# Two tile pairs in turn at the ends of the second layer and at the start of the output stage; split weights loaded whole

## The chip, the cores and the metric

The kernel runs on one core of one Trainium2 chip. The metric is device time in microseconds (us). Engines: PE (TensorE, matrix products), ACT (ScalarE), DVE (VectorE), POOL (GpSimd, here used to issue weight loads), SP (SyncE, which issues the other loads and stores). PE reads SBUF and accumulates in PSUM; ACT and DVE read the sums out of PSUM.

## The reference

Three stages in a row, on 1792 tokens (4 batches of 448), everything in float32:

```python
# attention, 48 (batch, head) pairs, seq 448, head_dim 64
scores = q @ k.T / sqrt(64) - log(448)
x = sigmoid(scores) @ v                      # gathered to x: 1792 x 768
# first layer: elementwise maximum of three products, then a projection
h = maximum(maximum(x @ w1, x @ w2), x @ w3) # 1792 x 768
y = h @ w_out                                # 768 x 768
# second layer and output
h2 = y @ w_in                                # 1792 x 1024
e = exp(h2 - max(h2)); solu = h2 * e / sum(e)
ln = (solu - mean) / sqrt(var + 1e-6) * g_ln # per token
out = ln @ w_out2                            # 1024 -> 768
```

The kernel multiplies `w_out @ w_in` once beforehand, so the second layer is one product of h with a 768 x 1024 matrix.

## The kernel before

**Products.** Each float32 operand is split into a high and a low half of a shorter format (a copy that rounds, then a subtraction), and each product is three matmuls: high x high, high x low, low x high. On top of that every large product uses the seven-product form of a 2 x 2 block multiplication: the left operand gives A11, A12, A22 and the combinations S1 to S4, the right one B11, B21, B22 and T1 to T4, and `PROD` (line 38) says which pair makes P1 to P7. The split right operands ("weights") are written to DRAM early (`w_d`, `w2_d`) and read back later.

**Stages.** First attention and the preparation of the weights, then the first layer in units of nine-matmul products (line 643), then the second layer, called L, then the output stage, called O. L and O each have seven *pairs* p = 0 to 6; a pair is two tiles of 128 tokens. In L a pair is 7 products of 9 matmuls with 512 columns, in O 7 products of 12 matmuls with 384 columns (line 909). L needs seven weights of 1.57 MB (`wf`, in order of use B11, B21, T2, T1, T3, T4, B22), O seven of the same size (`w2t`). They share SBUF slots, so an O weight can be loaded only when the last L pair has used the L weight in its slot (`release`, lines 1024 to 1029). O's B11 has a slot of its own and is loaded early.

**Operands of a pair.** `prep` (line 771) is a generator that makes the seven left operands of a pair step by step: ACT makes each high half (line 51), DVE each low half (line 56) and the sums and differences (line 59). The order is A11, A12, S2, S1, S3, A22, S4, the order in which P1, P2, P6, P5, P7, P4, P3 need them. They live in a ring of ten slots; an L operand takes one slot, an O operand two, and a slot is free once PE has used what lies in it. L's operands come from the rows of h in DRAM (`load_h`, on SP), O's from `u_d` (`load_u`, on SP).

**The order of products.** The loop of line 1058 does one pair after another: P1 of the new pair, then P4 and P3 of the pair before (`close`), then P2, P6, P5, P7 of the new one. P1, P6, P7 and P4 of a pair go into the same PSUM tile X: after each, ACT copies X out (lines 1065, 1109, 1115, 1044) before the next may add to it. P5 and P3 share V, P2 has Z. DVE adds the copies up (line 934 in L, line 59 in O).

**After an L pair** comes `solu_ln` (line 939): two Exp on ACT, two products on DVE, two Squares on ACT, a chain of small steps between ACT and DVE, two scalings on ACT (line 973), two transposes on DVE (line 977), and stores to `u_d`. O's pair p needs the result for p. `load_u(p)` also insists that pair p+1 is through.

**The written order.** PE, ACT, DVE and, late in the kernel, POOL run in program order; each executes its instructions in the order in which the program emits them. A planner decides where the side work goes (lines 880 to 922): each matmul earns credit (0.227 in L, 0.174 in O, line 906), each emitted step costs its planned time, and while credit is positive steps are taken from `bg` (the preps) and, if that has none, from `lazy` (the solu_ln). `charge` books the evacuations. Two places ignore credit: `product_c` takes prep steps until its operand exists, and `load_u` takes lazy steps until the pair is through:

```python
while t not in turned or (p + 1 < NP2 and tiles[2 * p + 3] not in turned and p > 0):
    assert step(lazy), t
```

**Weight loads.** POOL loads each L weight in three pieces of 0.5 MB and each O weight in four of 0.4 MB. Before each piece, `paced` (line 729) lets POOL copy a few values (line 732) of the piece issued three before, which makes POOL wait until that has landed. `w_d` rows are 4 KB per chunk.

**PSUM** has 2 tiles Z, 2 X, 2 V (lines 627 to 629).

Of the kernel before, what the change touches and what calls it, by code (L numbers as in the profile page):

```python
# [15 lines left out]
P = 128  # L16
# [28 lines left out]
def sigmoid_attention_max_moe_solu_ln(tc, q, k, v, w123, wo, wi, w2, g, out):  # L45
# [582 lines left out]
    px_cm, ps_x = open_pool("ps_x", 2, space=PSUM)  # L628
# [122 lines left out]
    spent, cops = set(), {}  # L751
# [18 lines left out]

    def prep(kind, p, a11, a12, a21, a22, s1, view, cost):
        ready = {}

        def high(nm, src):
            parts = halves_of((kind, p, nm))
            while parts is None:
# [3 lines left out]
            copy(act, view(parts[0]), src)  # L780

        def low(nm):
            src, parts = ready.pop(nm)
            rest(dve, view(parts[1]), src, view(parts[0]))
# [4 lines left out]
        yield from high("A12", a12)  # L789
        low("A11")  # L790
        yield cost
        tt(s1, a21, a22, ALU.add)
# [5 lines left out]
        tt(a11, s1, a11, ALU.subtract)  # L798
# [4 lines left out]
        yield from high("S1", s1)  # L803
        low("S2")
        yield cost
        yield from high("S3", a21)
        low("S1")
        yield cost
        yield from high("A22", a22)
        low("S3")  # L810
        yield cost
        yield from high("S4", a12)
        low("A22")
        yield cost
        low("S4")
        yield cost

    def prep_l(p):
        a = [hts.pop((p, i, k)) for i in range(2) for k in range(2)]
        s1 = f_tile(*FIN[8 + p % 2], f"s1_{p}")[:, :HU]  # L820
# [4 lines left out]
    for n, u in enumerate(units):  # L825
# [8 lines left out]
        if old is not None:  # L834
# [4 lines left out]
            if old["u"] == (NG - 1, 1):  # L839
# [14 lines left out]
        if n == len(units) - 1:  # L854
            bg.append(prep_l(0))
# [5 lines left out]
        if u == (NG - 1, 1):  # L861
# [6 lines left out]
            flow.extend(hts[(0, i, k)][:, :8] for i, k in ((1, 1), (0, 1), (1, 0)))  # L868
# [70 lines left out]
    def solu_ln(p):  # L939
# [4 lines left out]
        for i, t in enumerate(pair):  # L944
# [3 lines left out]
            yield 0.2  # L948
# [6 lines left out]
        for i in range(2):  # L955
            c = slice(i, i + 1)
            act.activation(e[i], h[i], AF.Square, bias=su[:, c], scale=-float(F2), accum_out=vs[:, c])
            yield 0.2
# [12 lines left out]
        for i in range(2):  # L971
            c = slice(i, i + 1)
            act.activation(h[i], h[i], AF.Identity, bias=nb[:, c], scale=s1[:, c])
            yield 0.2
# [16 lines left out]
    def prep_o(p):  # L991
# [6 lines left out]
        s1 = tp.tile([P, 4, P], F32, tag="s1", name=f"os1_{p}", bufs=1).rearrange("p k (i t) -> p k i t", i=4)  # L998
        return prep("O", p, *a, s1, lambda t: t.rearrange("p (k i t) -> p k i t", k=4, i=4), 0.69)

    spare = [("e", None)] * 3 + FIN[:4] + FIN[10:]
# [29 lines left out]
    def close(o):  # L1031

        kind, p = o["kind"], o["p"]
        e1, u2, u3, cx = o["at"]
# [8 lines left out]
        else:  # L1043
            act.copy(cx, o["X"])
            put_out(p, 1, 0, cx)
        product_c(o["V"], kind, p, "P3", False, True)
# [10 lines left out]
    stage = [("L", p) for p in range(NP2)] + [("O", p) for p in range(NP2)]  # L1057
    for n, (kind, p) in enumerate(stage):
        w = 512 if kind == "L" else HU
        at = targets(kind, p)  # L1060
        e1, u2, u3, cx = at
        X = ps_x.tile([P, 512], F32, tag="x", name=f"X{n}")[:, :w]
        product_c(X, kind, p, "P1", True, False)
        release(kind, p, "P1")
        act.copy(e1, X)
# [12 lines left out]
        else:  # L1078
            close(old)
        if n == 3:  # L1080
            load_w2(LOADS[0], 7)
        if 0 < n < NP2 - 1:
            load_h(p + 1, 0)
            load_h(p + 1, 1)
        if NP2 - 1 <= n + 1 < len(stage) - 1:
            load_u(n + 2 - NP2)
# [99 lines left out]
```

## Time and profile before

| | us |
|---|---|
| median of 3 runs (lowest, highest) | 705.95 (705.54, 709.5) |
| the profiled execution | 706.08 |
| its span, first to last instruction | 704.3 |
| PE busy | 656.2 (93%) |
| DVE busy | 491.4 (70%) |
| ACT busy | 372.7 (53%) |
| POOL busy | 83.2 (12%) |
| mean granted clock of PE | 0.966 |

The busy shares are means over stages. A row of a timeline is: start, duration, engine, line, operation, destination <- sources, shapes, count and, in brackets, the idle time of the engine ahead of it and what ended that. Names have no buffer numbers: X, V, Z are PSUM tiles, `wf` an L weight, `w2t` an O weight, c_L and c_O operands of a pair, `h`, `u`, `e`, `cx` the evacuated sums, `a` rows of h.

### The profile page before, as it was taken

Reading aid. Unit: us, or ns where it says so; the run is one execution under the profiler, and the core shown is the slowest. Engines: PE = TensorE matmul, PEld = TensorE weight load, DVE = VectorE, ACT = ScalarE, POOL = GpSimd, SP = SyncE. Lnnn points to the kernel's source line nnn. Section 1 sums busy time; section 2 is a strip of 40 time slices with the busy share of each in tenths; the row PEclk is TensorE's granted clock in tenths of the full one; section 3 lists DMA queues with packets and bytes.
Section 4 is the critical chain, followed back from the end, with each engine's and each line's share of the span. In section 5 each row is a group of like instructions: output and inputs, shape, how many; then the busy total and the mean of one; then the engine's idle time right before and its main releaser. Section 6 shows DMA issues by size and latency. Waiting matters only on the chain.

```text
span 704.3 us, 9779 instructions
## 1 busy us (share of the span) xinstructions
PE 656.2 (93%) x3283; PEld 528.7 (75%) x3283; DVE 491.4 (70%) x1061; ACT 372.7 (53%) x709; POOL 83.2 (12%) x184
## 2 busy tenths in 40 slices
PE   9999999999999999999999998579999958885997
PEld 6555688545569999999999997348888847884997
DVE  4799977797467888868976866227887835654652
ACT  6888333678665554555455533116667714735341
POOL 1111110001001011111011003330001431000000
PEclk9999999999999999999999999869999977988999
DMA  8788688736201556554675349982534797354311
GB/s 282 228 255 256 185 275 307 285 110 221 87 1 48 149 181 211 156 163 153 176 213 165 111 125 328 305 285 67 165 104 121 246 285 250 97 149 137 107 52 68
DMA packets 83201, 125.16 MB, mean 178 GB/s; under 512 B 35792, under 2 KB 62928, under 8 KB 83152
## 3 DMA queue, kind: packets, MB, share of 16 engines
q1 hardware_dynamic: 71344, 70.84, 32.1%
q0 software_dynamic: 11664, 53.49, 24.6%
q8 instruction: 26, 0.43, 0.3%
q14 instruction: 23, 0.19, 0.1%
q10 hardware_dynamic: 144, 0.23, 0.1%
HBM read 84.15 MB, written 40.37 MB: 177 GB/s over the span
## 4 chain that ended last, share of the span: by engine, by line
PE 55%; issue 14%; DMA 13%; DVE 12%; ACT 5%; POOL 1%; SPq 0%; POOLq 0%; DVEq 0%; ACTq 0%
PE x L643 17%; PE v L643 9%; PE av L272 7%; PE X L909 6%; DMA w2tT<-w_d 4%; PE z L643 4%; PE sc L251 4%; PE V L909 4%; DMA wfT<-w_dT 3%; DMA wfB<-w_dB 3%; PE sc L247 2%; PE Z L909 1%; DMA w2tB<-w_d 1%; DVE y_wo L157 1%; DVE wt L59 1%
## 5 line engine op out<-in xcount | busy, mean ns | idle before, releaser
L272 PE MATMUL av<-sf,vr 128*64 128x448 f32 x384 | 77.5, 545 | 0.0
L259 ACT ACTIVATE sf<-sc,bias_s 128x896 f32<-128x896 f32 x72 | 67.8, 1011 | 1.3
L141 POOL DMA_DIRECT2D raw<-in_w x52 | 28.2, 543 | 279.9 <-DVE S L56 140.1
L272 PEld LDWEIGHTS av<-sf,vr 128*64 128x64 f32 x384 | 25.4, 136 | 40.8 <-issue 35.5
L251 PE MATMUL sc<-qt,kt 64*128 64x448 f32 x432 | 52.0, 377 | 3.5 <-ACT sf L256 3.5
L251 PEld LDWEIGHTS sc<-qt,kt 64*128 64x128 f32 x432 | 38.5, 184 | 15.1 <-ACT sf L256 5.9
L472 PE MATMUL pw<-wi_t,r_wo 128*128 128x512 f32 x216 | 49.6, 390 | 0.0
L472 PEld LDWEIGHTS pw<-wi_t,r_wo 128*128 128x128 f32 x216 | 40.4, 188 | 9.3 <-issue 1.0
L683 ACT COPY u<-x 128x448 f32<-128x448 f32 x36 | 19.1, 531 | 43.3 <-PE x L643 43.3
L909 PE MATMUL X<-w2tT,c_O_S 128*128 128x384 f32 x168 | 35.0, 358 | 7.3 <-DMA w2tT<-w_d 7.3
L909 PE MATMUL X<-wfT,c_L_S 128*128 128x512 f32 x126 | 34.8, 420 | 6.7 <-DMA wfT<-w_dT 6.1
L909 PEld LDWEIGHTS X<-w2tT,c_O_S 128*128 128x128 f32 x168 | 31.7, 204 | 8.8 <-DMA w2tT<-w_d 7.2
L59 DVE TENSOR_TENSOR u<-V,u 128x384 f32<-128x384 f32 x14 | 7.8, 557 | 39.6 <-ACT u L1115 28.1
L909 PEld LDWEIGHTS X<-wfT,c_L_S 128*128 128x128 f32 x126 | 24.6, 200 | 14.4 <-DMA wfT<-w_dT 5.4
L643 PE MATMUL x<-T3h,S 128*128 128x448 f32 x108 | 33.7, 366 | 0.0
L643 PE MATMUL x<-B11h,A 128*128 128x448 f32 x108 | 33.7, 366 | 0.0
L643 PE MATMUL x<-T4h,A 128*128 128x448 f32 x108 | 33.6, 365 | 0.0
L643 PE MATMUL x<-T2h,S 128*128 128x448 f32 x108 | 33.6, 365 | 0.0
L643 PE MATMUL v<-B22h,S 128*128 128x448 f32 x108 | 33.6, 365 | 0.0
L643 PE MATMUL v<-T1h,S 128*128 128x448 f32 x108 | 33.6, 365 | 0.0
L643 PE MATMUL z<-B21h,A 128*128 128x448 f32 x108 | 33.6, 365 | 0.0
L412 ACT ACTIVATE raw<-raw,g_sb 128x192 f32<-128x192 f32 x32 | 13.3, 466 | 31.3 <-DVE raw L157 31.3
(187 smaller groups left out, 1597.6 us busy)
## 6 DMA issues: line engine op xcount, KB each, us to landing
raw<-in_w POOLq DMA_DIRECT2D x52, 384.0 KB, 4.1
w_d<-w2s SPq DMA_DIRECT2D x48, 192.0 KB, 2.4
u_d<-e SPq DMA_DIRECT2D x14, 512.0 KB, 2.8
ut<-u_d SPq DMA_DIRECT2D x56, 128.0 KB, 4.0
kr<-in_k SPq DMA_DIRECT2D x24, 256.0 KB, 3.3
vr<-in_v SPq DMA_DIRECT2D x24, 256.0 KB, 3.9
raw<-in_wi POOLq DMA_DIRECT2D x16, 384.0 KB, 4.5
w_dT<-wsT SPq DMA_DIRECT2D x12, 512.0 KB, 3.6
```

Source lines behind the costliest of these rows:

```text
L59: dve.tensor_tensor(out=dst, in0=a, in1=b, op=op)
L141: pool.dma_start(out=t, in_=source(key).rearrange("p (n t) -> p n t", t=2))
L157: dve.scalar_tensor_tensor(out=yi, in0=raws[key][:, cols, 0], scalar=29, in1=yi, op0=ALU.logical_shift_right, op1=ALU.bitwise_or)
L247: pe.matmul(sc[:, 0, :S], lhsT=kt[:, x, c * P :], rhs=qt[:, y], start=start, stop=stop)
L251: pe.matmul(sc[:, j, :S], lhsT=kt[rows, x, c * P : (c + 1) * P], rhs=qt[rows, y], start=start, stop=stop)
L259: act.activation(sf, sc[:, :, :S], AF.Sigmoid, bias=bias_s, scale=1.0 / math.sqrt(D))
L272: pe.matmul(pa[j * D : (j + 1) * D, :S], lhsT=vr[:, j, c], rhs=sf if c == 3 else sf[:, j], start=(n == 0), stop=(n == 3),)
L412: act.activation(half, half, AF.Copy, scale=g_sb[:, kc + 4 * i : kc + 4 * i + 1])
L472: pe.matmul(ps, lhsT=wt[:, a, cols], rhs=wi_t[:, b, c0 : c0 + 512], start=(i == 0), stop=(i == 3 * KC - 1))
L643: pe.matmul(ps, lhsT=l, rhs=r, start=(start and c == 0 and i == 0), stop=(stop and c == 2 and i == 2), skip_group_check=True)
L683: act.copy(e, ps)
L909: pe.matmul(ps, lhsT=hl[l][:, c * P : (c + 1) * P], rhs=wt[:, c, m], start=(start and c == 0 and i == 0), stop=(stop and c == chunks - 1 a ...
```

## The change

- **Pairs in turn.** The loop runs over groups: L (0,1), (2), (3), (4), (5,6) and O (0,1), (2), ... (6). In a group of two, each product is done for both pairs before the next product. The two preps are interleaved (`in_turn`), the first with a lead of 8, 6 or 1 steps. P4 of a group of two comes ahead of the next P1. X has three PSUM tiles.
- **Loads.** Each L weight is one DMA without gates. POOL waits only, by `hold`, for the h rows of pair 0 and of pair 1 before it issues weights behind them. O weights keep their four pieces; POOL waits for the piece four before.
- **load_u** takes one prep step ahead of each forced lazy step, and stands at other places: for pair 1 after P1 of (5,6), pair 2 after P1 of O (0,1), pair 3 after its P5, pairs 4 to 6 after P6 of O 2 to 4.
- **Costs and small things.** ACT steps of `solu_ln` are planned at 0.05 instead of 0.2. The s1 buffer of odd O pairs is two pieces, so its instructions are too. When the ring is full, `high` emits the pending low half before it waits.

```diff
-    px_cm, ps_x = open_pool("ps_x", 2, space=PSUM)
+    px_cm, ps_x = open_pool("ps_x", 3, space=PSUM)
...
-    def paced(out, in_):
-
-        if len(flow) > 2:
-            pool.tensor_copy(gate, flow.popleft())
-        pool.dma_start(out=out, in_=in_)
-        flow.append(out[:, 0, :8])
+    def hold(view):
+
+        pool.tensor_copy(gate, view)
...
-        for c in range(3):
-            paced(t[:, c].bitcast(F32), w_d[nm][:, c, : 2 * 512].rearrange("p (a b) -> p a b", a=2))
+        pool.dma_start(out=t.bitcast(F32).rearrange("p c a b -> p c (a b)"), in_=w_d[nm][:, :, : 2 * 512])
...
         for kc in range(4):
-            paced(t[:, kc].bitcast(F32), w2_d[n][kc][:, off])
+            if len(flow) > 3:
+                hold(flow.popleft())
+            pool.dma_start(out=t[:, kc].bitcast(F32), in_=w2_d[n][kc][:, off])
+            flow.append(t[:, kc, 0, :8].bitcast(F32))
...
+        def high(nm, src, before=None):
             parts = halves_of((kind, p, nm))
+            if parts is None and before:
+                low(before)
+                before = None
+                yield cost
+                parts = halves_of((kind, p, nm))
             while parts is None:
                 yield None
                 parts = halves_of((kind, p, nm))
             ready[nm] = (src, parts)
-            copy(act, view(parts[0]), src)
+            for d, t in pieces(view(parts[0]), src):
+                copy(act, d, t)
+            if before:
+                low(before)
...
+    def in_turn(first, second, lead):
+
+        gens, n = [first, second], 0
+        while gens:
+            for gen in gens[n % 2 :] + gens[: n % 2] if n >= lead else gens[:1]:
+                cost = next(gen, "end")
+                if cost == "end":
+                    gens.remove(gen)
+                    break
+                if cost is not None:
+                    n += 1
+                    yield cost
+                    break
+            else:
+                yield None
...
-                for tag in (2, 3, 4):
-                    load_wf(LOADS[tag], tag)
                 last_rows(1)
                 for k in range(2):
                     load_h(1, k)
+                for k in range(2):
+                    hold(hts[(1, 1, k)][:, :8])
+                for tag in (2, 3, 4):
+                    load_wf(LOADS[tag], tag)
...
-            bg.append(prep_l(0))
+            bg.append(in_turn(prep_l(0), prep_l(1), 8))
...
             act.activation(e[i], h[i], AF.Exp, bias=low[:, c], scale=-1.0, accum_out=ssum[:, c])
-            yield 0.2
+            yield 0.05
...
             while t not in turned or (p + 1 < NP2 and tiles[2 * p + 3] not in turned and p > 0):
+                step(bg)
                 assert step(lazy), t
...
+    groups = [("L", g) for g in ((0, 1), (2,), (3,), (4,), (5, 6))]
+    groups += [("O", g) for g in ((0, 1), (2,), (3,), (4,), (5,), (6,))]
+    prev = None
+    for n, (kind, g) in enumerate(groups):
+        if prev and len(prev) > 1:
+            for o in prev:
+                fourth(o)
+        now_open = [begin(kind, g[0])]
...
+            close(prev)
+        now_open += [begin(kind, p) for p in g[1:]]
-        if n == 3:
+        if n == 2:
             load_w2(LOADS[0], 7)
+        if (kind, g) == ("L", (5, 6)):
+            load_u(1)
+        elif (kind, g) == ("O", (0, 1)):
+            load_u(2)
+        elif kind == "L" and 2 <= g[0] < 5:
+            next_h(g[0] + 1)
+        last = n == len(groups) - 1
         if not last:
+            for o in now_open:
+                second(o)
+        for o in now_open:
+            sixth(o)
+        if (kind, g) == ("L", (0, 1)):
+            next_h(2)
+        elif (kind, g) == ("L", (4,)):
+            next_h(6)
+            load_u(0)
+            bg.append(in_turn(prep_l(5), prep_l(6), 6))
+        elif kind == "L" and g[0] < 4:
+            bg.append(prep_l(g[0] + 1))
+        elif (kind, g) == ("L", (5, 6)):
+            bg.append(in_turn(prep_o(0), prep_o(1), 1))
+        elif not last:
+            bg.append(prep_o(g[-1] + 1))
+            if 2 <= g[0] < 5:
+                load_u(g[0] + 2)
+        for o in now_open:
+            fifth(o)
+        if (kind, g) == ("L", (0, 1)):
+            bg.append(prep_l(2))
+        elif (kind, g) == ("O", (0, 1)):
+            load_u(3)
+        for o in now_open:
+            seventh(o)
...
+        prev = now_open
+    close(prev)
```

`begin`, `second`, `sixth`, `fifth`, `seventh`, `fourth`, `third` are the old loop's and `close`'s lines for P1, P2, P6, P5, P7, P4, P3 with their evacuations; `next_h(p)` takes prep steps until pair p-2 is prepared and then loads the h rows of pair p; `close` now does P4 only where the group before was a single pair, and P3 of each of its pairs.

## Rows read from the trace of the kernel before

**Rows 1.** Page part 2: PE's busy tenths in 40 slices of 17.6 us.

```profile
PE   9999999999999999999999998579999958885997
```

**Rows 2.** Busy by stage: PE, PEld, DVE, ACT, POOL, clock, DMA share, GB/s.

```profile
475.00:545.00 70.00, 70.00 (x303) 57.16 (x302) 56.11 (x127) 46.14 (x90) 1.20 (x3) 0.99 0.37 114
545.00:580.00 35.00, 27.69 (x126) 23.36 (x125) 21.70 (x44) 16.14 (x30) 14.96 (x35) 0.89 0.90 265
...
600.00:626.00 26.00, 20.81 (x102) 19.86 (x100) 15.45 (x30) 13.90 (x27) 0.00 (x0) 0.87 0.50 135
626.00:652.00 26.00, 17.05 (x84) 16.09 (x84) 13.83 (x27) 13.17 (x24) 0.00 (x0) 0.87 0.40 119
```

**Rows 3.** PE's timeline in L: start, us, line, tiles, count, idle before and releaser.

```profile
429.69 0.86 PE L909 MATMUL X<-wfB,c_L_A 128*128 128x512 f32 x3
...
473.60 3.62 PE L909 MATMUL Z<-wfB,c_L_A 128*128 128x512 f32 x9
477.05 2.26 PE L909 MATMUL X<-wfT,c_L_S 128*128 128x512 f32 x9
...
565.98 2.37 PE L909 MATMUL V<-w2tT,c_O_S 128*128 128x384 f32 x12
```

**Rows 4.** POOL's timeline: the gate copies and the first reload.

```profile
433.30 0.19 POOL L732 COPY gate<-wfB 128x8 f32<-128x8 f32 x1 [0.51 <-DMA wfB<-w_dB]
...
472.23 0.19 POOL L732 COPY gate<-wfB 128x8 f32<-128x8 f32 x1 [1.67 <-DMA wfB<-w_dB]
...
543.80 0.54 POOL L733 DMA_DIRECT2D w2tB<-w_d  x1 [69.29 <-PE X L909]
```

**Rows 5.** PE's timeline in O.

```profile
590.01 2.78 PE L909 MATMUL V<-w2tB,c_O_S 128*128 128x384 f32 x6 [0.98 <-DMA w2tB<-w_d]
...
596.26 2.24 PE L909 MATMUL X<-w2tT,c_O_S 128*128 128x384 f32 x12
...
612.93 0.51 PE L909 MATMUL V<-w2tT,c_O_S 128*128 128x384 f32 x2
617.51 3.57 PE L909 MATMUL V<-w2tT,c_O_S 128*128 128x384 f32 x10 [4.07 <-DVE c_O_S L56]
...
636.26 0.51 PE L909 MATMUL V<-w2tT,c_O_S 128*128 128x384 f32 x2
643.63 3.57 PE L909 MATMUL V<-w2tT,c_O_S 128*128 128x384 f32 x10 [6.86 <-DVE c_O_S L56]
...
658.37 2.24 PE L909 MATMUL Z<-w2tB,c_O_A 128*128 128x384 f32 x12
...
697.97 2.27 PE L909 MATMUL V<-w2tB,c_O_S 128*128 128x384 f32 x12
```

**Rows 6.** ACT's timeline in the middle of O.

```profile
631.62 1.15 ACT L947 ACTIVATE e<-h,st 128x1024 f32<-128x1024 f32 x1
...
638.89 2.37 ACT L973 ACTIVATE h<-h,st 128x1024 f32<-128x1024 f32 x2 [1.02 <-DVE st L969]
...
649.40 0.48 ACT L1115 COPY u<-X 128x384 f32<-128x384 f32 x1 [6.73 <-PE X L909]
```

**Rows 7.** Busy time and DMA share while the L weights arrive.

```profile
427.00:445.00 18.00, 12.43 (x54) 9.23 (x52) 9.34 (x18) 5.07 (x10) 4.79 (x14) 1.00 1.05 377
445.00:466.00 21.00, 15.57 (x44) 9.75 (x42) 6.21 (x13) 4.75 (x10) 8.85 (x23) 0.76 0.86 270
```

**Rows 8.** DMA queues from 445 to 466: packets, MB, share of 16 engines.

```profile
q0 software_dynamic: 1484, 5.37, 80.6%
```

**Rows 9.** DMA queue and issues, 427 to 445 (KB each, us to landing).

```profile
q1 hardware_dynamic: 3363, 2.29, 40.2%
...
a<-h_d SPq DMA_DIRECT2D x5, 192.0 KB, 7.4
```

**Rows 10.** SP's timeline: issues of h rows.

```profile
426.64 4.66 SPq L704 DMA_DIRECT2D a<-h_d  x3
```

**Rows 11.** DVE's timeline: the last low half of a chain.

```profile
651.59 0.69 DVE L56 TENSOR_TENSOR c_O_A<-ut,c_O_A 128x512 fp32r<-128x512 f32 x1
```

More of the change, by code (lines that the diff above doesn't have):

```diff
@@ L788, in prep @@
         yield 0.1
-        yield from high("A12", a12)
-        low("A11")
+        yield from high("A12", a12, "A11")
         yield cost
-        tt(s1, a21, a22, ALU.add)
+        for t, l, r in pieces(s1, a21, a22):
+            tt(t, l, r, ALU.add)
         yield cost
@@ L797, in prep @@
         yield cost
-        tt(a11, s1, a11, ALU.subtract)
+        for t, l, r in pieces(s1, a11, a11):
+            tt(r, t, r, ALU.subtract)
         yield cost
@@ L867, in sigmoid_attention_max_moe_solu_ln @@
             load_h(0, 1, slice(0, 2))
-            flow.extend(hts[(0, i, k)][:, :8] for i, k in ((1, 1), (0, 1), (1, 0)))
+            for k in range(2):
+                hold(hts[(0, 1, k)][:, :8])
             last_rows(0)
@@ L1045, in close, with third @@
             put_out(p, 1, 0, cx)
+    def third(o):
+        kind, p = o["kind"], o["p"]
+        u2 = o["at"][1]
         product_c(o["V"], kind, p, "P3", False, True)
@@ L1055, in close, with begin @@
             put_out(p, 0, 1, u2)
-    stage = [("L", p) for p in range(NP2)] + [("O", p) for p in range(NP2)]
-    for n, (kind, p) in enumerate(stage):
+    def close(units):
+        if len(units) == 1:
+            fourth(units[0])
+        for o in units:
+            third(o)
+    def begin(kind, p):
         w = 512 if kind == "L" else HU
         at = targets(kind, p)
-        e1, u2, u3, cx = at
-        X = ps_x.tile([P, 512], F32, tag="x", name=f"X{n}")[:, :w]
+        X = ps_x.tile([P, 512], F32, tag="x", name=f"X{kind}{p}")[:, :w]
@@ L1063, in sigmoid_attention_max_moe_solu_ln, with second @@
         product_c(X, kind, p, "P1", True, False)
         release(kind, p, "P1")
-        act.copy(e1, X)
+        act.copy(at[0], X)
+        return dict(kind=kind, p=p, X=X, at=at, w=w)
+    def second(o):
+        kind, p, e1 = o["kind"], o["p"], o["at"][0]
+        if kind == "L":
+            new_st(p)
+        Z = ps_z.tile([P, 512], F32, tag="z", name=f"Z{kind}{p}")[:, : o["w"]]
+        product_c(Z, kind, p, "P2", True, True)
+        release(kind, p, "P2")
+        if kind == "L":
+            add_min(e1, Z, e1, sts[p][0][:, :1], 3.0e38)
+        else:
+            tt(e1, Z, e1, ALU.add)
+            charge(0.56)
+            put_out(p, 0, 0, e1)
@@ new lines, in sixth, with fifth, seventh @@
+    def sixth(o):
+        product_c(o["X"], o["kind"], o["p"], "P6", False, False)
+        release(o["kind"], o["p"], "P6")
+        act.copy(o["at"][1], o["X"])
+    def fifth(o):
+        V = o["V"] = ps_v.tile([P, 512], F32, tag="v", name=f"V{o['kind']}{o['p']}")[:, : o["w"]]
+        product_c(V, o["kind"], o["p"], "P5", True, False)
+        release(o["kind"], o["p"], "P5")
+    def seventh(o):
+        kind, p, u3 = o["kind"], o["p"], o["at"][2]
+        product_c(o["X"], kind, p, "P7", False, False)
+        release(kind, p, "P7")
+        act.copy(u3, o["X"])
+        if kind == "L":
+            add_min(u3, o["V"], u3, sts[p][0][:, 1:], 3.0e38)
+        else:
+            tt(u3, o["V"], u3, ALU.add)
+            charge(0.56)
+            put_out(p, 1, 1, u3)
@@ L1066, in sigmoid_attention_max_moe_solu_ln, with next_h @@
+    def next_h(p):
+        while p >= 2 and ("L", p - 2) not in prepared:
+            assert step(bg)
+        for k in range(2):
+            load_h(p, k)
+    groups = [("L", g) for g in ((0, 1), (2,), (3,), (4,), (5, 6))]
[6 more added lines that the diff above has]
+        now_open = [begin(kind, g[0])]
         if n == 0:
```

92 lines of the change are left out of this document (32 added, 60 removed).

## The prediction

> **What bounds the kernel now.** I read the page's slices first. TensorE (PE) is at 9 tenths nearly everywhere and dips in two places only: slices 25 to 27 and slices 33 to 37 [rows 1]. The table by stage then separates them. Between 475 and 545 us PE is busy for all 70.0 us. In 545 to 580 it is busy for 27.7 of 35 us with DMA at 0.90, and in 600 to 652 for 37.9 of 52 us with DMA at 0.50 and 0.40 [rows 2]. So there are three holes: the start of the second layer (L), the start of the output stage (O), and the middle of O. Outside them PE sets the time.
>
> The PE timeline gives their size. L runs undisturbed from 477.05 to 565.98: 43 products in 88.93 us, so a product is 2.07 us [rows 3].
> - **L start.** From 429.69 to 473.60 (43.9 us) PE does eight L products and two first-layer products. At 2.07 and 1.81 us (448 columns instead of 512) that is 20.2 us, so 23.7 us are lost. The next product takes 3.45 instead of 2.07 us [rows 3]: 25.1 us in all. The cause is in POOL's queue: the copy that waits for the last piece of the first weight ends its wait at 433.30, that for the last piece of the seventh weight at 472.23 [rows 4], 6.49 us per weight against 2.07 us per product.
> - **O start.** From 565.98 [rows 3] to 596.26 there are six products, 12.4 us of work in 30.3 us: 17.8 us lost. The reload cannot begin before the last L pair has used each weight: the first issue is at 543.80 [rows 4], and PE still waits for the last piece (V<-w2tB) at 590.01 [rows 5].
> - **Middle of O.** From 612.93 to 658.37 there are twelve products, 24.9 us of work in 45.4 us: 20.5 us lost. PE stops at 617.51 for 4.07 us and at 643.63 for 6.86 us, both times on DVE's low half c_O_S [rows 5]. ScalarE (ACT) shows why: from 631.62 (Exp, L947) to 641.26 (end of L973) it works through a whole solu_ln block [rows 6], which load_u forces into the order. The operand copies and evacuations stand behind it.
>
> **The change, part by part.** Durations come from the one profiled execution (span 704.3, its time 706.08; the median shown is 705.95, 0.13 lower).
>
> *L start.* Each weight now serves two products, 4.14 us, before the next is wanted. Whole loads let no product start on a third of a weight, so P1 of pair 0 waits until about 433.3, where its last piece landed before. From there PE does ten L and two first-layer products: 433.3 + 20.7 + 3.65 = 457.6, when P4 of pair 0 wants weight six (T4). Then come P4, P4, P1 of pair 2, and P3 twice with weight seven (B22). When do these land? In 445 to 466 the DMA engines were only 0.86 busy, in 427 to 445 1.05 [rows 7]; with three pieces in flight the queue ran dry. POOL's queue moved 5.37 MB in 80.6% of 21 us [rows 8], so a weight of 1.57 MB needs 4.96 us when something always waits. The h rows and stores on the SP queue took 40.2% of 18 us beside it [rows 9]; until 445 they still need 4.7 us. So weight seven lands at 433.3 + (6 x 4.96 + 4.7) / 1.05 = 466.1 and weight six at 461.4. P4, P4, P1 end at 467.6 and P3 twice at 471.7. By then 15 L products are done; before, that point was 477.05 + 6 x 2.07 = 489.5 (nine were done at 477.05). Gain 17.8 us. The fast end is PE at pace from 457.6: 468.0, gain 21.5. The slow end is the landing of before, 472.23, plus 4.1: 476.4, gain 13.1. The Trainium skill (DMA: Bandwidth & Descriptors, § Bandwidth) gives 341 GB/s for a DMA of 1 MB and advises that size or more; by that an estimate is 4.6 us per weight, the gain nearer 20, the sum near 691. The trace has 317 GB/s for pieces of half a megabyte, so the two do not contradict each other, and no run here shows a larger transfer yet. I keep 17.8, since the h rows share the engines.
>
> The new hold stops the POOL queue, weights three to seven behind it, until pair 1's rows have landed. The third and fourth of their loads are among the issues of 426.64 to 431.3 [rows 10], 7.4 us to landing [rows 9]: 438.7 at the latest. Weight three is wanted at 433.3 + 3.65 + 4 x 2.07 = 445.2, 6.5 us later, which is just what one took before: nothing, or 1 us. The added split instructions (s1 in two pieces) and the third PSUM buffer lie beside PE and cost nothing there: in L's middle DVE was 56.1 of 70.0 us busy and ACT 46.1 [rows 2]. Without that cover it is one more low half, 0.7 us, per odd pair.
>
> Moved at no cost: the h rows of pairs 2 and 6 go out earlier on SP, whose next entries are rows of later pairs, and O's first weight, now loaded one stage sooner, still stands last in POOL's queue, far ahead of its use.
>
> *O start.* With pairs 5 and 6 in turn, the first weight is free with twelve L products still to come instead of eight, and O's first pair needs its weights at 4.14 us each. The reload took 543.80 to 590.01, 46 us; the seventh weight is now wanted 25 products (52 us) after the first release, the second 14 products (29 us). All 17.8 us go.
>
> *Middle of O.* What is late next is the order of ACT and DVE, and here the planner's own costs decide (lines 880 to 922). An L pair earns 63 x 0.227 = 14.3; its prep costs 11 x 0.56 + 0.1 = 6.3 and its charges 3.1, so 4.9 is left against 6.74 for one solu_ln with the new yields. Groups 2 to 4 pay for about 13 of it, so nothing of solu_ln(2) is out when load_u(1) demands it. An O pair earns 14.6 less 7.7 and 1.7 = 5.2. Each forced block and the prep steps taken with it leave a debt of 6 to 11, and nothing beyond need is issued until it is paid. So solu_ln(2) is forced whole in (5,6), (4) nearly whole behind P5 of O(0,1), (5) whole behind P6 of O2, (6) whole behind P6 of O3; load_u(6) forces nothing.
> - *The blocks.* (2) costs nothing: six products (12.4 us) lie before the first matmul that needs a copy queued behind it. The other three have three products, P5, P7 and the next P1 (or P5, P7, P7): 6.2 us. Then P4 writes X, which the copy of P7's result must have read, and that copy is behind the block on ACT. ACT's share of a block is 9.6 us [rows 6]; with a copy ahead of it (0.5), none, one or four interleaved operand copies (0.5 each) and the copy itself (0.5) the waits are 4.4, 4.9 and 6.4: 15.7 us.
> - *Operands issued on need.* In debt, an operand is issued only behind the evacuation of the product just done. At 649.40 ACT begins that copy, and the last low half ends at 651.59 + 0.69 [rows 6, 11]: 2.9 us from a copy, an add, two operand copies and three low halves. I count nine such places from P1 of O1 to P1 of O5 (P1 and P6 of O1, P4 of O1, P1 of O2, P2 and P6 of O3, P2 and P6 of O4, P1 of O5), and price each by how much of that chain it repeats: 2.5, 2.1, 1.5, 1.5, 1.2, 2.4, 1.6, 3.0, 2.8 = 18.6 us; the ends are one low half each, 6.2, and the whole chain each, 26.
> - *Clock.* After the 4.07 us stop the granted clock in that stretch is 0.87 [rows 2], between the levels 2.4 and 1.2 GHz. From 617.51 to 636.26 PE does 14.2 us of products in 18.75 [rows 5]. Of the 4.6 us I put 1.6 on an operand on need, 3.0 on the clock. Three blocks: 9.0 us.
>
> Together 43.3 us come where 20.5 went. **Sum:** 706.08 - 17.8 - 17.8 - 20.5 + 43.3 = 693.3; less the 0.13 and rounded, **693 us**. Bounds: loads 13.1 to 21.5; blocks 0 to three times the dearest hole of before (6.86, so 20.6); clock 0 to 14 (4.6 three times).
>
> **Rivals.**
> 1. *The blocks are hidden.* load_u now takes one prep step per solu_ln step, so the low halves on which PE stopped at 617.51 and 643.63 come out ahead of the block. If ACT is through with it within the 6.2 us, blocks and clock cost nothing and the 18.6 us on need stay: 706.1 - 35.6 - 20.5 + 18.6 = 668.6. Against it: 9.6 us of ACT do not fit into 6.2.
> 2. *Loads no faster.* If weights still land every 6.49 us, L gains 13.1: 698.0. For it: the engines were already full to 445 [rows 7].
> 3. *Operands never ahead (slower).* An O operand takes two of ten ring slots, so five operands serve two pairs. If from P1 of O1 to P1 of O5 (33 products) every product waits for its operand as the nine do, 18.6 / 9 = 2.07 us each, that is 68.3 us in place of the 18.6: 743; it decides from 31.3 us, 0.95 us per product, on: 706. I take half of it as the case: 34 + 15.7 + 9.0 = 59, 709. Against it: O5 and O6 of before, with the same ring, run nineteen products in the 39.6 us from 658.37 to 697.97 [rows 5].
>
> **Chances.** Forecast 0.47 (own range 683 to 701: 8 to 10 us either way, about a third of the blocks and the clock, 8.2, or the loads' slow end, 4.7), rival 1 0.26, rival 2 0.16, rival 3 0.11. 1% (7 us, 698.9 and 713.0) is about what a measurement here can tell from no change. Faster: 0.41 of the forecast, 0.26, 0.07 = 0.74. Same: 0.06, 0.09 and 0.04 of rival 3 = 0.19. Slower: the rest of rival 3, 0.07. The range goes from rival 1 to just above no change, 667 to 706, and leaves out rival 3 and the best of rival 1.
>
> **What would show it.** After the change the weight gates disappear and PE's stops on wfB and wfT between 433 and 472 shrink to under 6 us in sum; no PE stop names w2t. PE stops before P4 of O0, O2 and O3 with an ACT copy (the u copy of P7) as releaser, 4 to 7 us each, and shorter ones on c_O names. The forecast is wrong if those three stops are under 2 us (rival 1), if P3 of pair 1 ends later than 476 (rival 2), or if nearly every O product is preceded by a c_O wait (rival 3).

## The result and the profile after

The changed kernel takes 700.18 us (median of 4 runs, 699.38 to 700.64) against 707.62 us for the kernel before on the same chip (4 runs, 705.54 to 709.5): ratio 0.9894, 95% interval 0.9857 to 0.9932. That is faster by 1.1%, where 693 us were forecast. The profiled execution took 700.64 us, its span is 698.9 us against 704.3.

The page's slices (40 of 17.5 us) show PE's dip at slices 25 to 27 of [rows 1] nearly gone, and a longer row of dips from slice 31 to 38. The clock is lowest in slice 32.

```profile
PE   9999999999999999999999998899997887786797
...
PEclk9999999999999999999999999999999799988999
```

The table by stage, with the columns of [rows 2], puts a loss into L, where before there was none (PE 70.00 of 70 us in 475 to 545), and with it a DMA share of 0.56 instead of 0.37. In the middle of O PE is busy 35.91 of 52 us, against 37.86 before.

```profile
475.00:545.00 70.00, 63.84 (x270) 51.23 (x269) 51.39 (x117) 43.12 (x83) 11.58 (x28) 0.97 0.56 170
545.00:580.00 35.00, 31.33 (x149) 28.16 (x148) 21.90 (x49) 17.73 (x35) 7.81 (x20) 0.91 0.65 203
600.00:652.00 52.00, 35.91 (x164) 32.57 (x163) 27.64 (x54) 24.63 (x46) 0.00 (x0) 0.87 0.44 127
```

PE's timeline in L (columns as in [rows 3]; the two tiles of a pair in turn make a row of 18 matmuls) has two long stops on weights (a third, at 458.12, is 0.26 us), one of 0.93 us on an ACT copy of h at 509.04, and one of 5.18 us at L's end:

```profile
432.86 2.31 PE L948 MATMUL XL<-wfB,c_L_A 128*128 128x512 f32 x9 [3.19 <-DMA wfB<-w_dB]
...
447.79 5.96 PE L948 MATMUL XL<-wfT,c_L_S 128*128 128x512 f32 x18 [2.77 <-DMA wfT<-w_dT]
...
472.82 2.24 PE L948 MATMUL ZL<-wfB,c_L_A 128*128 128x512 f32 x9
...
519.77 4.28 PE L948 MATMUL ZL<-wfB,c_L_A 128*128 128x512 f32 x18
...
541.60 7.14 PE L948 MATMUL XL<-wfT,c_L_A 128*128 128x512 f32 x18 [5.18 <-ACT h L1148]
...
555.09 0.62 PE L948 MATMUL XO<-w2tB,c_O_A 128*128 128x384 f32 x2
```

At 472.82 fifteen L products are done; before, that point was 489.5 (the prediction's reckoning from [rows 3]). So the L start gained 16.7 us. From 519.77 to 555.09 there are 13 products, 26.9 us of work in 35.3: 8.4 us lost, where before L had no such stop.

The list of all that PE waited for (us in total, times, longest):

```profile
PE XO L948 <- ACT u L1148: 8.9, 3, 4.9
PE XO L948 <- ACT c_O_S L51: 6.2, 3, 2.6
PE XL L948 <- ACT h L1148: 5.2, 1, 5.2
PE XO L948 <- ACT c_O_A L51: 4.5, 4, 1.6
PE XO L948 <- DVE c_O_A L56: 3.9, 3, 1.7
...
PE XL L948 <- DMA wfT<-w_dT: 3.0, 2, 2.8
PE ZO L948 <- DVE c_O_A L56: 2.4, 2, 1.5
```

No row names w2t: the stall at O's start is gone. The rest of O, 48 products from 555.09 to 695.04, is 99.8 us of work in 139.95: 40.1 us lost, against 20.5 before in O's middle [rows 5] and 17.8 at its start. **Balance** of the spans: L start -16.7 (0.2 of it before L), O start -17.8, middle of O -20.5 + 40.1, L end + 8.4, the stop at 509.04 with the slower products behind it + 1.4, what follows the last product - 0.4. That is -5.5; the spans differ by 5.4.

The new stop at L's end is explained by ACT's timeline. The solu_ln blocks share three e buffers; the second Exp of solu_ln(3) needs the one that the first tile of solu_ln(2) held, whose store to u_d was issued at 532.37 and landed 7.4 us later. The copies of P7's results (L1148) stand behind it, and P4, which adds to the same X, waits for them.

```profile
533.41 1.15 ACT L986 ACTIVATE e<-h,st 128x1024 f32<-128x1024 f32 x1
...
539.84 1.15 ACT L986 ACTIVATE e<-h,st 128x1024 f32<-128x1024 f32 x1 [5.18 <-DMA u_d<-e]
...
540.99 1.05 ACT L1148 COPY h<-XL 128x512 f32<-128x512 f32 x2
```

The DMA issues (KB each, median us to landing) suggest why the store took so long. The first fence is the kernel before from 475 to 545, the second the changed one from 520 to 545, where the reload of the O weights runs beside them:

```profile
u_d<-e SPq DMA_DIRECT2D x6, 512.0 KB, 2.7
```

```profile
u_d<-e SPq DMA_DIRECT2D x3, 512.0 KB, 8.8
```

The reload alone does not fix the figure: in the kernel before, two stores issued at 560.82, beside its reload, landed in 6.3 us.

### The profile page after: what moved, and what is told of

It reads as the page before. It is cut to its first block, busy times and chain, and to the rows that moved or that the text cites. A ratio compares the mean times of both kernels' runs of the same rounds, so it can differ in the third digit from the quotient of the medians.

```text
span 698.9 us, 9717 instructions
## 1 busy us (share of the span) xinstructions
PE 651.9 (93%) x3283; PEld 526.4 (75%) x3283; DVE 490.7 (70%) x1070; ACT 372.4 (53%) x712; POOL 72.4 (10%) x149
## 4 chain that ended last, share of the span: by engine, by line
PE 56%; DVE 21%; DMA 8%; ACT 8%; issue 6%; SPq 1%; POOL 0%; DVEq 0%; ACTq 0%; POOLq 0%
PE x L643 18%; PE v L643 9%; PE XO L948 6%; PE z L643 4%; PE av L272 4%; PE XL L948 3%; PE VO L948 3%; PE sc L251 3%; DMA ut<-u_d 2%; PE ZO L948 2%; DMA a<-h_d 2%; ACT e L996 2%; DMA wfT<-w_dT 1%; DVE y_wi L157 1%; ACT h L1012 1%
## 5 line engine op out<-in xcount | busy, mean ns | idle before, releaser
L683 ACT COPY u<-x 128x448 f32<-128x448 f32 x36 | 19.1, 530 | 43.2 <-PE x L643 43.2
L948 PE MATMUL XO<-w2tT,c_O_S 128*128 128x384 f32 x168 | 32.4, 340 | 6.6 <-ACT c_O_S L51 6.2
L948 PE MATMUL XL<-wfT,c_L_S 128*128 128x512 f32 x126 | 32.4, 409 | 4.0 <-DMA wfT<-w_dT 3.0
L948 PEld LDWEIGHTS XO<-w2tT,c_O_S 128*128 128x128 f32 x168 | 29.0, 188 | 8.5 <-ACT c_O_S L51 7.2
L948 PEld LDWEIGHTS XL<-wfT,c_L_S 128*128 128x128 f32 x126 | 24.6, 197 | 10.6 <-issue 3.8
L157 DVE SCALAR_TENSOR_TENSOR raw<-raw 128x384 int32<-128x384 int32 x52 | 29.0, 557 | 1.1
```

What stands on the lines that cost most here:

```text
L157: dve.scalar_tensor_tensor(out=yi, in0=raws[key][:, cols, 0], scalar=29, in1=yi, op0=ALU.logical_shift_right, op1=ALU.bitwise_or)
L683: act.copy(e, ps)
L948: pe.matmul(ps, lhsT=hl[l][:, c * P : (c + 1) * P], rhs=wt[:, c, m], start=(start and c == 0 and i == 0), stop=(stop and c == chunks - 1 a ...
```

## The experiments

Theory after this reading: the two halves of the change add up; the L start is worth -16.7 us, the half at L's end and O's start costs what it saves, through the order of ACT and DVE (the planner's account) and through the store beside the reload. The rivals stand with each run. All times are medians, and each ratio is against the kernel before, timed on the same chip.

### The L start alone

Pairs 0 and 1 of L in turn, everything later as before:

```diff
-    groups = [("L", g) for g in ((0, 1), (2,), (3,), (4,), (5, 6))]
-    groups += [("O", g) for g in ((0, 1), (2,), (3,), (4,), (5,), (6,))]
+    groups = [("L", g) for g in ((0, 1), (2,), (3,), (4,), (5,), (6,))] + [("O", (p,)) for p in range(7)]
...
-            yield 0.05
+            yield 0.2
...
-                step(bg)
                 assert step(lazy), t
```

> Only the first half of the change: the pairs 0 and 1 of L in turn, whole loads of the split weight, the three holds; from pair 2 on everything as in the kernel before (single pairs, load_u at its old places, solu_ln without the interleaved prep steps). Theory T (the two halves add up: L start gains 16.7 us, the half at L's end and O's start loses what it gains): 16.7 under the kernel before, 689 to 693 us, so some 9 us under the changed kernel; PE waits at O start on w2t for about 18 us as before and at c_O_S in the middle of O as before. Rival R (the time won at L start is lost again at O start, because the reload cannot begin before the last pair has used the weights and DMA is then busy with other things): 700 us or more, the w2t wait over 25 us.

Measured: 732.62 us, ratio 1.0368 (1.0326 to 1.0411), **26 us slower**. Both expectations fell: the gain is not kept, and it is not lost on w2t either (3.9 us of waits in V). The L start itself is as fast as in the changed kernel: from the entry into L to the end of its fifteenth product it takes 43.8 us, there 43.2, before 59.8. Two rows show where the time goes, the wait list and the middle of O in the table by stage:

```profile
PE XO L948 <- ACT c_O_S L51: 18.3, 5, 10.1
PE ZO L948 <- DVE c_O_A L56: 12.1, 2, 10.6
```

```profile
600.00:652.00 52.00, 28.90 (x125) 27.41 (x125) 21.20 (x42) 21.86 (x39) 0.00 (x0) 0.73 0.33 103
```

PE is busy 56% of this stretch, DVE 41%, ACT 42% and the DMA engines 33%: none of them is full, they wait for each other. The granted clock is 0.73, against 0.87 before [rows 2], so the products also run slower. ACT's timeline has the beginnings of three solu_ln blocks in O:

```profile
571.45 1.15 ACT L986 ACTIVATE e<-h,st 128x1024 f32<-128x1024 f32 x1
...
605.47 1.15 ACT L986 ACTIVATE e<-h,st 128x1024 f32<-128x1024 f32 x1
...
637.85 1.15 ACT L986 ACTIVATE e<-h,st 128x1024 f32<-128x1024 f32 x1
```

After its last L product the kernel before begins two such blocks, one of them at 631.62 [rows 6]. Its first Exp in L stands at 474.63, when eight L products are done; here it stands at 476.60, when fourteen are, six products later in the order (this execution enters L 4.2 us later, so the times differ by less). Six products of credit that solu_ln could have used are spent, so one block more is owed when load_u asks for it. That is a reading of the trace; the cheaper account below tests it.

### The other half alone

L start as before, L pairs 5 and 6 and O pairs 0 and 1 in turn:

```diff
-    groups = [("L", g) for g in ((0, 1), (2,), (3,), (4,), (5, 6))]
+    groups = [("L", g) for g in ((0,), (1,), (2,), (3,), (4,), (5, 6))]
...
-        return prep("L", p, *a, s1, lambda t: t, 0.56)
+        return prep("L", p, *a, s1, lambda t: t, 0.42)
```

> The other half alone: L start as before (single pairs, gated pieces of half a megabyte, old load order), L pairs 5 and 6 and O pairs 0 and 1 in turn, load_u at the new places. One figure differs from the change, since this order needs it: an L operand is charged 0.42 instead of 0.56 in the planner's account, so solu_ln(2) and (3) can come out a little earlier. T: from the changed kernel's trace, O start -17.8, middle of O +19.6, L end +8.4, L middle +1.2, together +11.4 us over the kernel before: 715 to 719 us, or some 5 us less if the cheaper L operand takes the stop at L end away. Rival R (this half gains, what is lost comes from the L start): 695 us or less.

Measured: 694.46 us, ratio 0.9819 (0.9761 to 0.9877). The theory of adding halves fell here too, and its rival was met: this half gains by itself, though with an L operand charged less than in the change, and of the waits on c_O names 4.3 us are left. A stop of 4.91 us before P4 of pair 5 is there.

### Without the store

One store to u_d, that of pair 2's first tile, is left out; the loads that read it read the second tile's.

```diff
-            sp.dma_start(out=u_d[t].rearrange("i f r e -> (i f) (r e)"), in_=ub)
+            if t != tiles[4]:
+                sp.dma_start(out=u_d[t].rearrange("i f r e -> (i f) (r e)"), in_=ub)
...
-                in_=u_d[t][:, :, r].rearrange("i f e -> f i e")
+                in_=u_d[tiles[5] if t == tiles[4] else t][:, :, r].rearrange("i f e -> f i e")
```

> The changed kernel without the store of pair 2's first u tile; the loads that read it read the second tile's u instead (as many bytes), so O's operands of pair 2 are partly another tile's. It takes away the one transfer on which the Exp of solu_ln(3)'s second tile waits for its buffer (three e buffers). T (the stop of 5.2 us before P4 of pair 5 is this buffer, held by a store that takes 8.8 us to land beside the reload): the Exp starts about 5 us sooner, the stop before P4 of pair 5 falls under 1.5 us, the low clock behind it goes too: 5 to 8 us under the changed kernel, 692 to 695 us. Rival R (ACT is late anyway, with the solu_ln block ahead of the u3 copy): the stop stays over 3.5 us and the time within 2 us.

Measured: 691.25 us, ratio 0.9773 (0.9729 to 0.9817), 8.9 us under the changed kernel's 700.18 (8.5 by the ratios), a little more than the 5 to 8 expected. The Exp follows its neighbour without a gap, and P4 of pair 5 runs at full pace:

```profile
537.45 4.39 PE L948 MATMUL XL<-wfT,c_L_A 128*128 128x512 f32 x18
```

The 13 products at L's end take 27.3 instead of 35.3 us, and the waits in O are the same as in the changed kernel (u copies 9.1 us, c_O_S 6.2). So of the 8.4 us at L's end 8.0 are this one buffer and store: **shown**. That the store lands late because of the reload is not shown by this run; the next one bears on it.

### Two pieces of the reload in flight

With the cheaper account of the next part:

```diff
-            if len(flow) > 3:
+            if len(flow) > 1:
```

> The changed kernel with the cheaper account, and in the reload of the O weights two pieces in flight instead of four. Its stop of 11.9 us before P4 of pair 5 is ACT waiting for a u_d store beside the reload. T (the store waits behind pieces of the reload that are already queued): stores land in 5 us instead of 8 to 9, the stop falls under 7 us, 676 to 681 us. Rival R1 (the store gets its share of the engines whatever is queued): the stop stays over 10 us, 683 to 687. Rival R2 (the reload becomes late): PE waits over 5 us for w2t at the start of O, 688 us or more.

Measured: 686.24 us against 684.83 with four in flight (ratios 0.9733, 0.9691 to 0.9774, and 0.9698, 0.9647 to 0.9748): no difference. The stores of 515 to 575 land in 5.5 instead of 7.8 us and the stop falls from 11.92 to 8.96, less than the theory asked for; in return PE waits 5.9 us for w2t. The two about cancel. So the number of pieces in flight bears on the landing of the stores, but none of the three expectations was met as a whole. The Trainium skill (DMA: Bandwidth & Descriptors, § Queues, rings and completion order) says that each DMA engine takes turns between the queues that have work, a packet at a time. By that, fewer pieces queued beside the store should change little as long as the queue is never empty. The slices of 0.5 us from 528 to 548 show the engines nearly idle for 2.5 us from 540.5 on, so the queue did run empty with two pieces, and this run does not decide on the rule:

```profile
DMA  8997999997999999998899999410009697958999
```

### The account

The planner books less for a prep step. Only the order of emission changes; the instructions are the same.

```diff
-        return prep("L", p, *a, s1, lambda t: t, 0.56)
+        return prep("L", p, *a, s1, lambda t: t, 0.42)
...
-        ... lambda t: t.rearrange("p (k i t) -> p k i t", k=4, i=4), 0.69)
+        ... lambda t: t.rearrange("p (k i t) -> p k i t", k=4, i=4), 0.50)
```

On the changed kernel:

> The changed kernel with two numbers of the planner changed: an L operand is charged 0.42 instead of 0.56 and an O operand 0.50 instead of 0.69, so that each product pays for more steps, solu_ln comes out in small portions behind the products and operands are issued ahead of need. No instruction is added or left out; only their order on ACT and DVE changes. T (the loss at L end and in the middle of O is the order: forced solu_ln blocks on ACT and operands issued on need): the PE waits on the u copies (8.9 us in sum, and 5.2 at L end) go below 4 us in sum and those on c_O names (17 us in sum) below 8: 675 to 685 us. Rival R (DVE and ACT have no room left there, the order does not matter): within 4 us of the changed kernel, 697 to 704, with the waits at other places but of the same sum.

Measured: 684.83 us, ratio 0.9698 (0.9647 to 0.9748). Order it is, by 15.4 us (13.8 by the ratios). The waits on u copies in O are gone, those on c_O names fall from 17.2 to 7.9 us. The time is at the upper edge of what the theory gave, since the stop at L's end grew, which the theory had shrink; the wait list shows it:

```profile
PE XL L948 <- ACT h L1148: 15.4, 4, 11.9
PE ZO L948 <- ACT c_O_A L51: 4.4, 1, 4.4
```

On the kernel before, the L start alone, and the other half alone:

> The kernel before with the cheaper account (an L operand charged 0.42, an O operand 0.50), nothing else. With the next two runs and the changed kernel with the same account (684.8 us) it makes a table of two halves by yes and no, in which solu_ln is not forced by the account. T (the middle of O of before, 20.5 us, was forced order): 684 to 692 us, the O start wait on w2t still about 18 us. Rival R (that hole is not the account's): 702 to 708.

> The L start alone once more, with the cheaper account. The L start alone came out 26 us slower than before; its trace shows solu_ln(3) to (6) each forced as one block in O0 to O2 and the end of L. T (pairs 0 and 1 in turn let the first solu_ln begin only after 15 L products instead of 9, so that with the old account one block more is still owed when load_u asks for it; where the account pays, the 16.7 us of the L start remain): 14 to 17 us under the kernel before with the same account, some 668 to 678 us. Rival R (the lost overlap of ACT and DVE with the six products of the L start costs its time whatever the account): not under the kernel before with the same account, stops of 6 us and more on c_O_S again.

> The other half (pairs 5 and 6 of L and 0 and 1 of O in turn, L start as before) with the cheaper account. T (the halves add up where the account pays): the w2t wait of about 18 us goes, the u_d store that holds an e buffer beside the reload costs 5 to 12: 8 to 15 us under the kernel before with the same account, some 674 to 682 us. Rival R (no gain beyond the account): within 4 us of the kernel before with the same account.

| | L's end and O's start singly | in turn |
|---|---|---|
| old account, L start singly | 705.55 to 707.62 (before) | not run (694.46 with an L operand at 0.42) |
| old account, L start in turn | 732.62 | 700.18 (changed) |
| cheaper account, L start singly | 701.47 (0.9953, 0.9921 to 0.9985) | 693.71 (0.9851, 0.9803 to 0.9898) |
| cheaper account, L start in turn | **672.96** (0.9557, 0.9512 to 0.9603) | 684.83 |

Everything in the column "in turn" has the new solu_ln steps and load_u of the change too.

The kernel before gains 4 us from the account (theory: 14 to 22; missed). The hole in the middle of O was the account's all the same: the waits on c_O names fall from 14.3 to 1.4 us. But L, which ran undisturbed before, now loses 12.6 us in the 43 products of [rows 3], 9.0 of them in waits on ACT's copies of h, and O's start 22.0 instead of 17.8:

```profile
PE X L909 <- ACT h L1115: 5.3, 5, 2.2
...
PE X L909 <- DVE c_O_A L56: 1.4, 1, 1.4
```

The other half gains 7.8 us on top of that (theory 8 to 15). The L start alone goes from 732.62 to 672.96: **60 us from the order alone**, and 28.5 us under the kernel before with the same account, more than the 14 to 17 expected. The two traces are 31 us apart: 15.4 at the L start, as expected, 6.5 less lost in the rest of L and 9.1 less at O's start (12.9 us lost there); why these two come with it was not tested. Its table row for the middle of O, to be set beside the one of the L start with the old account, has PE at 50.57 of 52 us:

```profile
600.00:652.00 52.00, 50.57 (x290) 49.94 (x289) 39.06 (x71) 29.00 (x56) 0.00 (x0) 1.00 0.54 157
```

So the 26 us were the order, as read; that it was just one block more was not tested by itself. With this account the second half, in the form of the change, takes 11.9 us back. The last four runs ask which part of it.

### Which part takes it back

All start from the L start with the cheaper account (672.96 us).

Weights in gated pieces:

```diff
-        pool.dma_start(out=t.bitcast(F32).rearrange("p c a b -> p c (a b)"), in_=w_d[nm][:, :, : 2 * 512])
+        for c in range(3):
+            if len(wflow) > 2:
+                hold(wflow.popleft())
+            pool.dma_start(out=t[:, c].bitcast(F32), in_=w_d[nm][:, c, : 2 * 512].rearrange("p (a b) -> p a b", a=2))
+            wflow.append(t[:, c, 0, :8].bitcast(F32))
```

> The L start alone with the cheaper account (672.96 us), with each split weight loaded in three gated pieces of half a megabyte again instead of whole. T (the step of the prediction that the queue moves a weight in 4.96 instead of 6.49 us when something always waits): the seventh weight lands as in the kernel before, P3 of pair 1 ends some 4 us later, 676 to 679 us. Rival R (with two products per weight the landing is not what ends last, whole or in pieces): within 2 us of 673.

Measured: 674.65 us, ratio 0.955 (0.9505 to 0.9595) against 0.9557 whole: the same. The whole loads do move faster. The table rows are the changed kernel's, then this one's:

```profile
445.00:466.00 21.00, 17.97 (x71) 14.11 (x71) 7.45 (x20) 5.00 (x11) 4.48 (x7) 0.92 1.05 394
```

```profile
445.00:466.00 21.00, 16.99 (x60) 12.09 (x61) 4.57 (x12) 3.79 (x8) 8.47 (x22) 0.92 0.90 300
```

394 against 300 GB/s, and 270 before [rows 7]. The Trainium skill (DMA: Bandwidth & Descriptors, § Bandwidth) asks for a megabyte or more per DMA. These rows are in line with it, but the whole loads also have no gates, so the size alone was not tested. And P3 of pair 1 ends at 472.8 whole in the changed kernel and at 474.3 in pieces, where the next product begins: with two products per weight, the landing hardly ends last any more.

```profile
474.29 2.24 PE L953 MATMUL ZL<-wfB,c_L_A 128*128 128x512 f32 x9
```

Then one end in turn at a time, both with solu_ln and load_u as before the change:

```diff
+    groups = [("L", g) for g in ((0, 1), (2,), (3,), (4,), (5,), (6,))]     # O's start in turn
+    groups += [("O", g) for g in ((0, 1), (2,), (3,), (4,), (5,), (6,))]
...
+    groups = [("L", g) for g in ((0, 1), (2,), (3,), (4,), (5, 6))]         # L's end in turn
+    groups += [("O", (p,)) for p in range(7)]
```

> The L start with the cheaper account, and of the other half only O's pairs 0 and 1 in turn; L's pairs 5 and 6 one after the other. Both halves together came out at 684.8 us, 11.9 over the L start alone. T (the loss sits at L's end, where the pairs in turn put solu_ln and its u_d stores beside the reload): no stop over 3 us before P4 in L, the 6.2 us of waits on w2t and the low clock behind them go: 663 to 670 us. Rival R (O's pairs in turn cost it: twice the operands early, nothing left for solu_ln): 680 us or more.

> The L start with the cheaper account, and of the other half only L's pairs 5 and 6 in turn; O one pair after the other. T (the loss sits at L's end): a stop of 5 us or more before P4 of pair 5, behind an Exp that waits for a u_d store: 680 to 688 us. Rival R (L's end is harmless, O's pairs in turn cost it): 668 to 676 us, with the w2t waits gone.

Measured: 667.16 us (0.9461, 0.9401 to 0.952) and 669.6 us (0.9494, 0.9438 to 0.9549). Neither end costs anything: of the first run the theory was met, of the second its rival. In both the waits on w2t are gone. L's end has its stop, 4.81 us before P4 of pair 5, but its releaser is the copy of P7's result behind a whole solu_ln block, in which no instruction waits for a store:

```profile
544.69 5.94 PE L948 MATMUL XL<-wfT,c_L_A 128*128 128x512 f32 x18 [4.81 <-ACT h L1147]
```

What both runs had and the changed kernel had not is the old solu_ln, so this was put under both ends:

```diff
-            yield 0.05
+            yield 0.2
...
-                step(bg)
                 assert step(lazy), t
...
+        elif kind == "O" and 2 <= g[0] < 5:
+            load_u(g[0] + 2)
...
-            if 2 <= g[0] < 5:
-                load_u(g[0] + 2)
```

> Both halves with the cheaper account (684.8 us), with the third part of the change undone: solu_ln's portions are charged 0.2 instead of 0.05 again, load_u takes no prep step between them and stands at its old place in O's pairs. L's end in turn alone gave 669.6 and O's start in turn alone 667.2, both with this old solu_ln. T (the third part is what costs: charged 0.05, solu_ln runs ahead of its e buffers and ACT stops behind an Exp that waits for a u_d store): at most three Exps wait for a u_d store, no stop over 6 us before P4 of pair 5: 660 to 669 us. Rival R (the two ends in turn disturb each other whatever solu_ln is charged): 680 to 687 us.

Measured: 668.17 us (6 runs, 666.46 to 668.65), ratio 0.9458 (0.9424 to 0.9493), against 684.83 with the new solu_ln: 16.7 us. What ACT waits for points at the cause, first with the new, then with the old solu_ln:

```profile
ACT e L986 <- DMA u_d<-e: 14.7, 5, 5.8
```

```profile
ACT e L986 <- DMA u_d<-e: 5.0, 3, 1.8
```

With the new solu_ln, ACT runs ahead of its e buffers and stands still at an Exp, with the copies that PE needs behind it in program order. These waits account for 9.7 us of ACT. The stop before P4 of pair 5 is 11.92 against 5.56:

```profile
558.72 6.52 PE L948 MATMUL XL<-wfT,c_L_A 128*128 128x512 f32 x18 [11.92 <-ACT h L1148]
```

```profile
544.62 7.09 PE L948 MATMUL XL<-wfT,c_L_A 128*128 128x512 f32 x18 [5.56 <-ACT h L1147]
```

That the three edits of this part cost the 16.7 us together is shown; they were not separated, so that it is the charge of 0.05 is argued. The same part under the old account was not run.

**The best versions** are this one and O's start in turn alone, 668 and 667 us, 5.4% under the kernel before; L's end in turn alone, 670 us, cannot be told from them. Both ends together are no better than either.

## Why the prediction was right or wrong

- **Sign and size.** Faster was right. 693 was 7 us low, and of the sum one term was missing and others were off by less: 693.3 + 1.1 (L start) - 3.2 (middle of O) + 8.4 (L's end) + 1.4 (L's middle) - 0.4 (behind the last product) = 700.6, the profiled execution's time.
- **L start, 17.8.** Measured 16.7, inside 13.1 to 21.5. The reason was half wrong. "A weight of 1.57 MB needs 4.96 us when something always waits" is borne out as a rate (POOL's queue moved 6.82 MB in the 21 us from 445 to 466, 4.8 us per weight), but in pieces P3 of pair 1 ends only 1.5 us later; two products per weight did the rest.
- **The hold.** Nothing or 1 us was said. POOL did wait 11.15 us in the first hold on pair 1's rows, and PE's stop before weight three (P6) is 2.77 us, so the size was short by about 2.
- **O start, 17.8.** All of it went. But the step stopped there, and its price was left out: a reload that runs inside L shares the DMA engines with the stores of solu_ln. The three e buffers did not appear in the prediction at all.
- **The step that failed: "(2) costs nothing: six products (12.4 us) lie before the first matmul that needs a copy queued behind it."** The block of solu_ln(2) itself did cost nothing: it ends at 530.8 and PE does not stop. But the order went straight on into solu_ln(3), for which the working names no place and no price, and its second Exp waited 5.18 us for the store, with the copies behind it. Taking the store away gave 8.9 us back, and the forecast was missed by 7. ACT's row for the end of solu_ln(2) in the changed kernel:

```profile
528.43 2.38 ACT L1012 ACTIVATE h<-h,st 128x1024 f32<-128x1024 f32 x2 [1.02 <-DVE st L1008]
```

- **The blocks, 15.7.** Three stops before P4 with the u copy as releaser, at the places named, O0, O2 and O3. They are 2.20, 4.89 and 1.79 us, 8.9 in sum; the middle one is as worked out (4.9), the other two are half of what was worked out (4.4) and under a third (6.4). Before the last one, P1 had already stopped twice on its own operand (0.75 and 1.43 us), while ACT got on with the block (from 626.86); why the first is shorter stays open. These are the rows of the changed kernel:

```profile
582.16 2.36 PE L948 MATMUL XO<-w2tT,c_O_A 128*128 128x384 f32 x12 [2.20 <-ACT u L1148]
...
611.63 4.21 PE L948 MATMUL XO<-w2tT,c_O_A 128*128 128x384 f32 x12 [4.89 <-ACT u L1148]
...
632.89 3.55 PE L948 MATMUL XO<-w2tB,c_O_A 128*128 128x384 f32 x10 [1.43 <-DVE c_O_A L56]
638.22 2.98 PE L948 MATMUL XO<-w2tT,c_O_A 128*128 128x384 f32 x12 [1.79 <-ACT u L1148]
```

- **Operands on need, 18.6.** The waits on c_O names sum to 17.2.
- **Clock, 9.0.** What is left of the 40.1 us, 14.0, is products that ran longer: P4 of O2 takes 4.21 us behind its stop, an undisturbed one 2.24; the granted clock of those 4 us is 0.50, the lower level. The sum of the three, 43.3, was 3.2 high, and in part by luck: the blocks were 6.8 too dear and the clock 5.0 too cheap.
- **Rivals.** Blocks hidden (668.6): no, the stops are there. Loads no faster (698.0): its time is the closest of all, its mechanism is not what happened, since P3 of pair 1 ended at 472.8, not after 476. Operands never ahead: no, the last products from 663.8 to 693.0 run undisturbed.
- **What the sum hid.** It adds an L start of -17.8 to an O priced for the whole change. The runs show that the L start has no price of its own: +26 us with the old account, -28.5 with the cheaper one. The sum came out near because the middle of O had been worked out for the whole change, with no solu_ln done early; this is argued from the working.

## What to carry to other kernels

Grouping work at the front of a stage puts off everything that waits for a finished tile; look at what the side work owes at the end of the stage before booking the gain. Where a planner's account sets an in-order engine's sequence, its costs are a part of the kernel: try them first, since here two numbers were worth 60 us in one arrangement and 4 in another. A step that is made cheap in the account can be issued too early, and an early step that waits for a buffer stops everything behind it on its engine; count the buffers and the landing time of what frees them.

## What the runs showed of the hardware

- Stores of 512 KB to DRAM landed in 2.7 us (median of 6) in L of the kernel before, nearly all without the reload, and in 8.8 us (median of 3) beside it in the changed kernel; loads of 128 KB from u_d went from 4.0 to 11.0 us. With two pieces of the reload in flight instead of four the stores took 5.5 instead of 7.8 us.
- With whole weights of 1.5 MB POOL stood in its issue with nothing waited for, before the fifth, sixth and seventh weight:

```profile
447.97 0.76 POOL L735 DMA_DIRECT2D wfT<-w_dT  x1 [6.57 <-issue]
452.46 0.77 POOL L735 DMA_DIRECT2D wfT<-w_dT  x1 [3.73 <-issue]
458.30 0.76 POOL L735 DMA_DIRECT2D wfB<-w_dB  x1 [5.08 <-issue]
```

  So about two such loads were outstanding at a time, without any gate in the program; what holds the third back was not tried.
- After PE's stop of 5.18 us at L's end the granted clock was 0.59 and 0.56 in the two stretches of 4 us from 540 on and 1.00 from 548, between the levels 1.2 and 2.4 GHz: the pair of products there took 7.14 instead of 4.28 us. So the stop cost 2.9 us more than its length.

```profile
540.00:544.00 4.00, 2.40 (x6) 1.92 (x7) 2.42 (x6) 2.55 (x5) 1.59 (x5) 0.59 1.06 319
544.00:548.00 4.00, 4.00 (x12) 3.13 (x11) 1.41 (x5) 0.00 (x0) 2.11 (x7) 0.56 0.90 298
```
